# Batch 0's tokens by TensorE transposes in place of a DMA transpose, and the block sums of the second weight all on VectorE

## The chip, the cores and the metric

The kernel runs on one core of one Trainium2 chip. The metric is the device time of one execution in microseconds (us), as the median of several executions. The kernel before has 280.86 us (three executions, 280.64 to 281.7). A profiled span is about 1.8 us shorter than the measured time of the same execution (278.6 against 280.41 us before); I compare spans with spans and times with times.

## The reference

Linear attention over 8 batches, 8 heads, 576 positions and 64 columns a head, then a layer norm and a two-layer network with a residual:

```python
q_s = softmax(q, axis=-1)          # over the 64 columns of a head
k_s = softmax(k, axis=2)           # over the 576 positions
kv  = einsum('bhsd,bhse->bhde', k_s, v)
att = einsum('bhsd,bhde->bhse', q_s, kv)
x   = att.transpose(0, 2, 1, 3).reshape(8, 576, 512)
xn  = (x - mean(x)) / sqrt(var(x) + 1e-6) * g_ln
out = x + maximum(xn @ w_ch1, 0) @ w_ch2     # 512 -> 2048 -> 512
```

## The kernel before

Every instruction is entered into a plan with its engine, an estimated length, the buffers that it reads and writes, and a class. The plan then puts each engine's instructions into one fixed order.

The network works on nine groups of 512 tokens: 512 of each of the 8 batches, and the eight leftovers of 64. For each group there is a first stage, 64 matmuls of 512 columns (`xsT` by `w1`, the result rectified into `hT`), and a second stage. Batch 0's second stage is the plain product, 64 matmuls of 512 columns. From batch 1 on, seven block products of 256 columns take the place of eight; they need block sums of `hT` (called `S`) and of the second weight (called `T`). All of this fills TensorE; the softmax of the next batch runs beside it on ScalarE and VectorE, and its small matmuls (`ek` by `vb`, `eqT` by `kve`) are strewn in between.

The attention leaves x transposed (`xsT`: columns in the partitions, tokens along the row), as the first stage wants it. The statistics and the residual want tokens in the partitions. A DMA transpose makes that form:

```python
def tokens(c, cls=1, after=(), stats=()):
    ...
    i = plan.add("SP", 2.2, lambda: nc.sync.dma_start_transpose(x.rearrange("p j (k c) -> p (j k) c", k=KO1), src.rearrange("p n t -> p (n t)")),
             r=r, w=[(xk, j) for j in range(J)], mb=0.9, land=0.6, after=after)
    for j in range(J):
        ... bn_stats and bn_aggr of x[:, j, :] on VectorE
    ... 1/sqrt(var) on ScalarE, by a logarithm and an exponential
```

Batch 0's transpose is issued behind batch 1's transpose of the softmax of q (`eqT<-eq`), since transposes are kept one after the other:

```python
gate[1] = dma_t()
state["eqT"] = gate[1], tokens(0, 0.7, (gate[1],))
```

The block sums of the second weight are four kinds of subtraction. One kind (`i == 2`) runs on GpSimd and is held back by a dummy copy until batch 0's output is begun:

```python
eng, e = ("POOL", nc.gpsimd) if i == 2 else ("DVE", nc.vector)
plan.add(eng, 1.2 if i == 2 else dve_t(256 * n, 2), lambda: e.tensor_tensor(T[i][:, ks], a, b, op=ALU.subtract),
         r=r + (["hold"] if i == 2 else []), w=tk(i), cls=2, after=after if i == 2 else ())
```

The softmax here doesn't subtract the row's maximum and nothing guards it: scores larger than these inputs give would overflow.

Of the kernel before, what the change touches and what calls it, by code (L numbers as in the profile page):

```python
# [12 lines left out]
FP32 = mybir.dt.float32  # L13
FP16 = mybir.dt.float16
# [3 lines left out]
ALU = mybir.AluOpType  # L18
# [116 lines left out]
def dve_t(n, mode=1):  # L135
    return 0.15 + n / (960.0 * mode)
# [3 lines left out]
def kernel(  # L140
# [10 lines left out]
    nc = tc.nc  # L151
# [3 lines left out]
    P = 128  # L155
    J = 4
# [4 lines left out]
    KO1 = DM // P  # L161
# [8 lines left out]
    def sb(shape, dt, name):  # L170
        return persist.tile(shape, dt, name=name, tag=name)
# [12 lines left out]
    eq = [sb([P, 2, JT, P], BF16, f"eq{i}") for i in range(2)]  # L184
    eqT = [sb([P, 2 * JT, P], BF16, f"eqT{i}") for i in range(2)]
    kve = [sb([P, G, D], FP16, f"kve{i}") for i in range(2)]
    hold = sb([P, 1], FP32, "hold")
    xb = [sb([P, J, DM], FP16, f"x{i}") for i in range(3)]
    x8 = sb([P, J, DM], FP16, "x8")
    xsT = [sb([P, J * KO1, P], FP16, f"xsT{i}") for i in range(2)]  # L190
# [3 lines left out]
    ot = [sb([P, 2, DM], FP32, f"ot{i}") for i in range(NOT)]  # L194
# [5 lines left out]
    T = [sb([P, HK, 256], FP16, f"T{i}") for i in range(4)]  # L200
# [3 lines left out]
    bst = sb([P, J, 6], FP32, "bst")  # L204
# [10 lines left out]
    def nxt(what, n):  # L215
        i = cnt[what] % n
        cnt[what] += 1
        return i
# [82 lines left out]


    ident_b = sb([P, P], BF16, "ident_b")
    plan.add("POOL", 1.5, lambda: make_identity(nc, ident_b), w=["ident"])
    XK = lambda u: [("xsT", u, j, g) for j in range(J) for g in range(G)]
    SLACK = 0.8
    EK = lambda u: [("eqT", u, i) for i in range(3)]

    def attn(b, kind, between=None, exps=(), sums_=(), kvs=()):
# [152 lines left out]
        if steady:  # L462
            state["eqT"] = (dma_t(),)
        else:
            gate[1] = dma_t()
            state["eqT"] = gate[1], tokens(0, 0.7, (gate[1],))
        for hf in range(2):
            keys(hf, lk[hf])
            values(hf, lv[hf])
# [10 lines left out]
    def tokens(c, cls=1, after=(), stats=()):  # L480

        x, xk, sti, stk = xof(c)
        if c < B:
            src, r = xsT[c % 2], XK(c % 2)
        else:
            src, r = xT8, [("xT8", b, i) for b in range(B) for i in range(2)]
        i = plan.add("SP", 2.2, lambda: nc.sync.dma_start_transpose(x.rearrange("p j (k c) -> p (j k) c", k=KO1), src.rearrange("p n t -> p (n t)")),
                 r=r, w=[(xk, j) for j in range(J)], mb=0.9, land=0.6, after=after)
        for j in range(J):
            plan.add("DVE", dve_t(512), lambda j=j: nc.vector.bn_stats(bst[:, j, :], x[:, j, :]), r=[(xk, j)], w=[("bst", j)], cls=cls, slack=2.0 if c else 0.5, after=stats)  # L490
            plan.add("DVE", 0.18, lambda j=j: nc.vector.bn_aggr(bmv[:, j, :], bst[:, j, :]), r=[("bst", j)], w=[("bmv", j)], cls=cls)
        plan.add("ACT", 0.3, lambda: nc.scalar.activation(sti[:, 3, :], bmv[:, :, 1], AF.Ln, bias=eps, scale=GS * GS),
                 r=["eps"] + [("bmv", j) for j in range(J)], w=[(stk, "v", j) for j in range(J)], cls=0)
        state["rstd"] = plan.add("ACT", 0.2, lambda: nc.scalar.activation(sti[:, 4, :], sti[:, 3, :], AF.Exp, scale=-0.5),
                 r=[(stk, "v", j) for j in range(J)], w=[(stk, "r", j) for j in range(J)], cls=0)
        return i


# [58 lines left out]
        tt(3, h12, S[1][:, ks], ALU.subtract, sk(1) + hi)  # L557
        tt(2, h11, h21, ALU.subtract, lo)

    def w2_sums(k0, n, after):  # L560

        ks, kh = slice(k0, k0 + n), slice(HK + k0, HK + k0 + n)
        b11, b12 = w2_sb[:, ks, 0:256], w2_sb[:, ks, 256:512]
        b21, b22 = w2_sb[:, kh, 0:256], w2_sb[:, kh, 256:512]
        lo, hi = [("w2", k0 + i) for i in range(n)], [("w2", HK + k0 + i) for i in range(n)]
        tk = lambda i: [("T", i, k0 + j) for j in range(n)]
        def tt(i, a, b, r):
            eng, e = ("POOL", nc.gpsimd) if i == 2 else ("DVE", nc.vector)
            plan.add(eng, 1.2 if i == 2 else dve_t(256 * n, 2), lambda: e.tensor_tensor(T[i][:, ks], a, b, op=ALU.subtract),  # L569
                     r=r + (["hold"] if i == 2 else []), w=tk(i), cls=2, after=after if i == 2 else ())  # L570
        tt(0, b12, b11, lo)
        tt(1, b22, T[0][:, ks], hi + tk(0))
        tt(2, b22, b12, lo + hi)
        tt(3, b21, T[1][:, ks], hi + tk(1))
# [97 lines left out]
    def mm2(c):  # L672

        gis = [nxt("pg", 4) for _ in range(J)]
        ids = []
        steps = [(8, 1), (8, 3), (12, 1)]
        for k0 in range(0, KO2, 4):
            for j in range(J):
                def f(k0=k0, j=j):
                    for kk in range(k0, k0 + 4):  # L680
                        nc.tensor.matmul(pg[gis[j]], hT[:, kk, j * P : j * P + P], w2_sb[:, kk, :],  # L681
                                         start=(kk == 0), stop=(kk == KO2 - 1))
                i = plan.add("PE", 0.864, f, r=[("hT", kk) for kk in range(k0, k0 + 4)] + [("w2", kk) for kk in range(k0, k0 + 4)], w=[("pg", gis[j])])
                if j == 0:
                    ids.append(i)
                if (k0, j) in steps:
                    second_x(steps.index((k0, j)), (i,))
        plan.fill(ids[0], ids[-1], zeros(pg[gis[0]], False))
        evs = []
        for hf in range(2):  # L690
            o = nxt("ot", NOT)
            for i in range(2):
                j = 2 * hf + i
                ev = plan.add("DVE", dve_t(512), lambda o=o, i=i, j=j: nc.vector.scalar_tensor_tensor(  # L694
                    ot[o][:, i, :], in0=pg[gis[j]], scalar=st[c % 3][:, 4, j : j + 1], in1=xb[c % 3][:, j, :],
                    op0=ALU.mult, op1=ALU.add),
                    r=[("pg", gis[j]), (("x", c % 3), j), (("st", c % 3), "r", j)], w=[("ot", o, i)], cls=0)
                evs.append(ev)
            store(c, o, hf)
        return evs[:1]  # L700

    def zeros(bank_, start):
        def f(n):
# [36 lines left out]
    for b in range(B):  # L740
        if b:
            state["tok"] = tokens(b, 0.7, stats=state["stats"])
        if b == B - 1:
            tokens(8, 0.7, stats=state["stats"])
        ids = mm1(b, b > 0, () if b else opened)
        if b == 0:
            plan.fill(warmed, open_ids[0], zeros(pg[3], True))
            plan.fill(open_ids[-1], ids[0], zeros(pg[opened[0]], False))
        elif b < B - 1:
            attn(b + 1, "steady", None, before, (ids[0],), (ids[10],))  # L750
        before = (ids[-1], state["rstd"])
        if b == 0:
            evs = mm2(b)
            plan.add("POOL", 0.2, lambda: nc.gpsimd.tensor_copy(hold, ot[0][:, 0, :1]), r=[("ot", 0, 0)], w=["hold"])
            for k0 in range(0, HK, 2):
                w2_sums(k0, 2, evs)
        else:
            mm2_split(b)
    mm1(8, True)
    mm2_split(8)  # L760

# [35 lines left out]
```

## Time and profile before

| | before |
|---|---|
| median time | 280.86 us |
| profiled span | 278.6 us |
| TensorE busy | 270.5 us, 97% |
| VectorE busy | 198.9 us, 71% |
| GpSimd busy | 5.9 us, 2% |

TensorE's timeline of the kernel before shows where its stages begin. The columns of a timeline are start, length, engine, line and operation, output and inputs, shape, count, and in brackets the idle time before with what ended it.

```profile
24.25 1.91 PE L538 MATMUL pg<-xsT,w_sb 128*128 128x512 f16 x8 [0.38 <-DVE w_sb L288]
...
36.35 8.80 PE L681 MATMUL pg<-w_sb,hT 128*128 128x512 f16 x40
...
46.87 1.04 PE L681 MATMUL pg<-w_sb,hT 128*128 128x512 f16 x4
47.84 0.63 PE L398 MATMUL pa<-eqT,kve 64*64 64x512 bf16 x8
...
66.96 0.60 PE L618 MATMUL pg<-w_sb,hT 128*128 128x256 f16 x4
...
67.83 3.22 PE L618 MATMUL pg<-w_sb,hT 128*128 128x256 f16 x28
71.00 1.49 PE L618 MATMUL pg<-T,S 128*128 128x256 f16 x12
72.41 0.83 PE L370 MATMUL pa<-vb,ek 64*64 64x65 f16 x72
...
83.14 7.08 PE L538 MATMUL pg<-xsT,w_sb 128*128 128x512 f16 x32
```

Batch 0's second stage begins at 36.35 us, batch 1's first stage at 52.15 us (in the prediction), its second stage at 66.96 us, and batch 2's first stage at 83.14 us.

VectorE's timeline shows the wait for the tokens and what follows it:

```profile
51.31 0.69 DVE L490 BATCH_NORM_STATS2 bst<-x 128x6 f32<-128x512 f16 x1 [3.77 <-DMA x<-xsT]
...
55.21 2.73 DVE L694 SCALAR_TENSOR_TENSOR ot<-pg,st,x 128x512 f32<-128x512 f32 x4 [0.60 <-ACT st L494]
...
73.81 0.88 DVE L628 SCALAR_TENSOR_TENSOR cp<-pg,st,x 128x256 f32<-128x256 f32 x2 [0.60 <-ACT st L494]
```

The last line is the evacuation that TensorE's 1.50 us hole at 74.75 us waits for (an evacuation is VectorE's or ScalarE's copy of a result out of PSUM, the memory that TensorE writes to).

### The profile page before, as it was taken

The numbers are of one execution on the slowest core, as the hardware profiler recorded it, in microseconds if no ns is written. First come the engines' busy times: TensorE is split into PE (matmuls) and PEld (weight loads), VectorE is DVE, ScalarE is ACT, GpSimd is POOL, SyncE is SP. The second block draws the span as 40 slices with busy tenths as digits, with TensorE's granted clock in tenths as the row PEclk, the third lists the DMA queues.
The fourth block names the chain that finished last, engine by engine and source line by source line (L and its number), as shares of the span: only waits on it lengthen the run. The fifth ranks groups of instructions, "written<-read, shape, count | busy, mean of one in ns | idle before, by whom it ended". The sixth has DMA issues, their size and how long they took to land.

```text
span 278.6 us, 5657 instructions
## 1 busy us (share of the span) xinstructions
PE 270.5 (97%) x2327; PEld 164.5 (59%) x2327; DVE 198.9 (71%) x406; ACT 167.9 (60%) x273; POOL 5.9 (2%) x15
## 2 busy tenths in 40 slices
PE   8999999999799999999999999999999999999994
PEld 3444444436674478447844784478447844874583
DVE  1878896599859966976599569764996773641572
ACT  4668986499478695668566946685655077016500
POOL 1000000060000000000000000000000000000000
PEclk9999999999999999999999999999999999999999
DMA  7999999998977993579858975697543450023004
GB/s 268 362 386 387 387 390 197 266 354 217 356 229 151 227 383 64 151 165 383 125 152 154 393 125 151 142 388 144 153 85 73 80 153 0 0 49 104 0 2 152
DMA packets 57953, 55.35 MB, mean 199 GB/s; under 512 B 36676, under 2 KB 37192, under 8 KB 57928
## 3 DMA queue, kind: packets, MB, share of 16 engines
q1 hardware_dynamic: 57776, 54.86, 68.2%
q8 instruction: 18, 0.29, 0.4%
q10 hardware_dynamic: 152, 0.13, 0.1%
q14 instruction: 7, 0.06, 0.1%
HBM read 36.70 MB, written 9.44 MB: 166 GB/s over the span
## 4 chain that ended last, share of the span: by engine, by line
PE 78%; DVE 13%; DMA 6%; ACT 2%; issue 1%; SPq 0%
PE pg L538 38%; PE pg L618 32%; DMA stg<-in_moe_w_ch_dram 4%; PE pg L705 3%; DVE eq L332 2%; DMA x<-xsT 2%; DVE S L554 2%; DVE zq L328 2%; DVE bst L490 2%; PE pa L370 1%; PE pa L618 1%; PE pa L398 1%; DVE ot L694 1%; DVE T L569 1%; PE pa L282 1%
## 5 line engine op out<-in xcount | busy, mean ns | idle before, releaser
L501 ACT ACTIVATE hT<-pg 128x512 f16<-128x512 f32 x134 | 78.8, 600 | 66.6 <-PE pg L538 65.7
L538 PE MATMUL pg<-xsT,w_sb 128*128 128x512 f16 x488 | 108.2, 379 | 1.1 <-ACT hT L501 0.4
L538 PEld LDWEIGHTS <-w_sb 128*128 128x128 f16 x568 | 54.9, 98 | 66.0 <-issue 1.4
L618 PEld LDWEIGHTS <-S 128*128 128x128 f16 x512 | 49.7, 98 | 7.6 <-issue 1.5
L618 PE MATMUL pg<-T,S 128*128 128x256 f16 x368 | 42.2, 273 | 1.5 <-DVE cp L628 1.5
L618 PEld LDWEIGHTS <-hT 128*128 128x128 f16 x384 | 37.0, 98 | 8.2 <-issue 3.0
L554 DVE TENSOR_TENSOR S<-hT 128x1024 f16<-128x1024 f16 x32 | 21.8, 683 | 23.6 <-ACT hT L501 23.6
L628 DVE SCALAR_TENSOR_TENSOR cp<-pg,st,x 128x256 f32<-128x256 f32 x46 | 20.2, 479 | 13.3 <-PE pg L618 12.6
L490 DVE BATCH_NORM_STATS2 bst<-x 128x6 f32<-128x512 f16 x36 | 24.1, 671 | 7.6 <-DMA x<-xsT 7.6
L618 PE MATMUL pg<-w_sb,hT 128*128 128x256 f16 x248 | 29.4, 273 | 0.0
L628 DVE SCALAR_TENSOR_TENSOR ot<-pg,st,cp 128x256 f32<-128x256 f32 x47 | 20.5, 476 | 11.4 <-PE pg L618 11.3
L332 DVE TENSOR_TENSOR eq<-eq,rzq 128x1152 bf16<-128x1152 bf16 x16 | 22.7, 1418 | 0.5
L328 DVE TENSOR_REDUCE zq<-eq 128x18 f32<-128x1152 bf16 x16 | 21.5, 1344 | 0.3 <-ACT eq L326 0.3
L359 ACT CAST vb<-stg 128x1152 f16<-128x1152 f32 x16 | 18.7, 1169 | 4.3 <-DMA stg<-in_v_dram 4.3
L326 ACT ACTIVATE eq<-stg 128x1152 bf16<-128x1152 f32 x16 | 18.8, 1176 | 2.1 <-DMA stg<-in_q_dram 1.9
L353 ACT ACTIVATE ek<-stg 128x1152 bf16<-128x1152 f32 x16 | 18.7, 1166 | 2.2 <-DMA stg<-in_k_dram 2.2
L411 ACT CAST xsT<-pa 128x512 f16<-128x512 f32 x30 | 15.5, 600 | 3.0 <-PE pa L398 3.0
L705 PE MATMUL pg<-zero 128*128 128x512 f16 x52 | 14.6, 430 | 1.2 <-DVE zero L224 1.2
L618 PE MATMUL pg<-w_sb,S 128*128 128x256 f16 x128 | 15.3, 272 | 0.0
L618 PE MATMUL pg<-T,hT 128*128 128x256 f16 x120 | 14.4, 272 | 0.4 <-DVE ot L628 0.4
L681 PE MATMUL pg<-w_sb,hT 128*128 128x512 f16 x64 | 14.7, 380 | 0.0
L538 PE MATMUL pg<-xT,w_sb 128*128 128x512 f16 x64 | 14.0, 379 | 0.0
(64 smaller groups left out, 164.6 us busy)
## 6 DMA issues: line engine op xcount, KB each, us to landing
stg<-in_q_dram SPq DMA_DIRECT2D x16, 576.0 KB, 5.3
stg<-in_k_dram SPq DMA_DIRECT2D x16, 576.0 KB, 7.3
stg<-in_v_dram SPq DMA_DIRECT2D x16, 576.0 KB, 8.2
out_dram<-ot SPq DMA_DIRECT2D x33, 256.0 KB, 3.5
stg<-in_moe_w_ch_dram SPq DMA_DIRECT2D x16, 512.0 KB, 9.7
out_dram<-ot SPq DMA_DIRECT2D x1, 512.0 KB, 2.8
x<-xsT SPq DMA_TRANSPOSE x8, 6.9
out_dram<-ot SPq DMA_DIRECT2D x1, 128.0 KB, 2.7
```

Of the source, the lines that this page charges most:

```text
L326: plan.add("ACT", act_t(QW), lambda: nc.scalar.activation(e.rearrange("p j (s d) -> p s j d", s=2), sv(s), AF.Exp), r=sk(s), w=[("eq", u, ...
L328: plan.add("DVE", dve_t(QW), lambda: nc.vector.reduce_sum(zq[:, hf], eh, axis=AX.X), r=[("eq", u, hf)], w=[("zq", hf)], cls=qcls, after=sums_)
L332: plan.add("DVE", dve_t(QW), lambda: nc.vector.tensor_tensor(eh, eh, rzq[:, hf].to_broadcast([P, 2 * JT, D]), op=ALU.mult), r=[("rzq", hf) ...
L353: plan.add("ACT", act_t(QW), lambda: nc.scalar.activation(ek[u][:, hf].rearrange("p j (s d) -> p s j d", s=2), sv(s), AF.Exp), r=sk(s), w= ...
L359: plan.add("ACT", act_t(QW), lambda: nc.scalar.copy(vd, va), r=sk(s), w=[("vb", u, hf, i) for i in range(2)], cls=cls, slack=late, after=t ...
L490: plan.add("DVE", dve_t(512), lambda j=j: nc.vector.bn_stats(bst[:, j, :], x[:, j, :]), r=[(xk, j)], w=[("bst", j)], cls=cls, slack=2.0 if ...
L501: nc.scalar.activation(hT[:, m, :], bank, AF.Relu)
L538: nc.tensor.matmul(bank[gi], w1_sb[:, ko, m * P : m * P + P], xt[:, ko], start=(ko == 0), stop=(ko == KO1 - 1))
L554: plan.add("DVE", dve_t(256 * n, 2), lambda: nc.vector.tensor_tensor(S[i][:, ks], a, b, op=op), r=r, w=sk(i), cls=0.3 if k0 else 0.45)
L618: nc.tensor.matmul(g[i][0], fa(k, i), fb(k), start=(first and k == 0 and (i == 0 or g[0][1] != g[1][1])), stop=(last and k == HK - 1), ski ...
L628: nc.vector.scalar_tensor_tensor(dst[:, i, :], in0=g[i][0], scalar=sti[:, 4, 2 * t0 + i : 2 * t0 + i + 1], in1=src[:, i, :], op0=ALU.mult, ...
L705: nc.tensor.matmul(bank_, zero[:, :P], zero, start=start, stop=start, skip_group_check=True)
```

## The change

The intent is to have batch 0's tokens earlier. TensorE transposes `xsT` itself, 16 blocks of 128x128 inside batch 0's second stage, and VectorE copies them out of PSUM. The DMA queue is rid of one transpose. GpSimd's block sums move to VectorE, so that they no longer contend with it. The core of the diff:

```diff
+    ident_h = sb([P, P], FP16, "ident_h")
+    plan.add("POOL", 1.5, lambda: make_identity(nc, ident_h), w=["ident_h"])
...
             gate[1] = dma_t()
-            state["eqT"] = gate[1], tokens(0, 0.7, (gate[1],))
+            state["eqT"] = (gate[1],)
...
-        i = plan.add("SP", 2.2, lambda: nc.sync.dma_start_transpose(...), ...)
+        for hf in range(2) if c == 0 else ():
+            t = nxt("pa", 4)
+            v = pa[t].bitcast(FP16)
+            def f(hf=hf, v=v):
+                for n in range(8):
+                    nc.tensor.transpose(v[:, n * P : n * P + P], src[:, 8 * hf + n, :], ident_h)
+            plan.add("PE", 0.52, f, r=r + ["ident_h"], w=[("pa", t)], cls=0, after=after)
+            plan.add("DVE", dve_t(1024, 2), lambda hf=hf, v=v: nc.vector.tensor_copy(
+                x[:, 2 * hf : 2 * hf + 2, :], v.rearrange("p (j n) -> p j n", j=2)), ...)
+        if c:
+            i = plan.add("SP", 2.2, lambda: nc.sync.dma_start_transpose(...), ...)
...
-            eng, e = ("POOL", nc.gpsimd) if i == 2 else ("DVE", nc.vector)
-            plan.add(eng, ..., lambda: e.tensor_tensor(T[i][:, ks], a, b, op=ALU.subtract), ...)
+            plan.add("DVE", dve_t(256 * n, 2), lambda: nc.vector.tensor_tensor(T[i][:, ks], a, b, op=ALU.subtract), ...)
...
+                if (k0, j) == (4, 2):
+                    tokens(0, 0.7, (i,))
```

The dummy copy `hold` and its ordering are removed too. The diff also sets the plan's slack for batch 0's statistics to 0, and passes on batch 0's 1/sqrt(var) as an ordering mark from its new place; both only move instructions. Because the plan orders everything anew, other instructions than these change places as well.

More of the change, by code (lines that the diff above doesn't have):

```diff
@@ L186 @@
     kve = [sb([P, G, D], FP16, f"kve{i}") for i in range(2)]
-    hold = sb([P, 1], FP32, "hold")
     xb = [sb([P, J, DM], FP16, f"x{i}") for i in range(3)]
@@ L486, in tokens @@
             src, r = xT8, [("xT8", b, i) for b in range(B) for i in range(2)]
-        i = plan.add("SP", 2.2, lambda: nc.sync.dma_start_transpose(x.rearrange("p j (k c) -> p (j k) c", k=KO1), src.rearrange("p n t -> p (n t)")),
-                 r=r, w=[(xk, j) for j in range(J)], mb=0.9, land=0.6, after=after)
+        i = None
+        for hf in range(2) if c == 0 else ():
[6 more added lines that the diff above has]
+            plan.add("DVE", dve_t(1024, 2), lambda hf=hf, v=v: nc.vector.tensor_copy(
+                x[:, 2 * hf : 2 * hf + 2, :], v.rearrange("p (j n) -> p j n", j=2)), r=[("pa", t)], w=[(xk, 2 * hf), (xk, 2 * hf + 1)], cls=cls)
+        if c:
+            i = plan.add("SP", 2.2, lambda: nc.sync.dma_start_transpose(x.rearrange("p j (k c) -> p (j k) c", k=KO1), src.rearrange("p n t -> p (n t)")),
+                     r=r, w=[(xk, j) for j in range(J)], mb=0.9, land=0.6, after=after)
         for j in range(J):
-            plan.add("DVE", dve_t(512), lambda j=j: nc.vector.bn_stats(bst[:, j, :], x[:, j, :]), r=[(xk, j)], w=[("bst", j)], cls=cls, slack=2.0 if c else 0.5, after=stats)
+            plan.add("DVE", dve_t(512), lambda j=j: nc.vector.bn_stats(bst[:, j, :], x[:, j, :]), r=[(xk, j)], w=[("bst", j)], cls=cls, slack=2.0 if c else 0.0, after=stats)
             plan.add("DVE", 0.18, lambda j=j: nc.vector.bn_aggr(bmv[:, j, :], bst[:, j, :]), r=[("bst", j)], w=[("bmv", j)], cls=cls)
@@ L494, in tokens @@
         state["rstd"] = plan.add("ACT", 0.2, lambda: nc.scalar.activation(sti[:, 4, :], sti[:, 3, :], AF.Exp, scale=-0.5),
-                 r=[(stk, "v", j) for j in range(J)], w=[(stk, "r", j) for j in range(J)], cls=0)
+                                 r=[(stk, "v", j) for j in range(J)], w=[(stk, "r", j) for j in range(J)], cls=0)
         return i
@@ L558, in sums, with w2_sums @@
         tt(2, h11, h21, ALU.subtract, lo)
-    def w2_sums(k0, n, after):
+    def w2_sums(k0, n):
         ks, kh = slice(k0, k0 + n), slice(HK + k0, HK + k0 + n)
@@ L567, in tt @@
         def tt(i, a, b, r):
-            eng, e = ("POOL", nc.gpsimd) if i == 2 else ("DVE", nc.vector)
-            plan.add(eng, 1.2 if i == 2 else dve_t(256 * n, 2), lambda: e.tensor_tensor(T[i][:, ks], a, b, op=ALU.subtract),
-                     r=r + (["hold"] if i == 2 else []), w=tk(i), cls=2, after=after if i == 2 else ())
+            plan.add("DVE", dve_t(256 * n, 2), lambda: nc.vector.tensor_tensor(T[i][:, ks], a, b, op=ALU.subtract),
+                     r=r, w=tk(i), cls=2)
         tt(0, b12, b11, lo)
@@ L688, in mm2 @@
         plan.fill(ids[0], ids[-1], zeros(pg[gis[0]], False))
-        evs = []
         for hf in range(2):
@@ L693, in mm2 @@
                 j = 2 * hf + i
-                ev = plan.add("DVE", dve_t(512), lambda o=o, i=i, j=j: nc.vector.scalar_tensor_tensor(
+                plan.add("DVE", dve_t(512), lambda o=o, i=i, j=j: nc.vector.scalar_tensor_tensor(
                     ot[o][:, i, :], in0=pg[gis[j]], scalar=st[c % 3][:, 4, j : j + 1], in1=xb[c % 3][:, j, :],
@@ L697, in mm2 @@
                     r=[("pg", gis[j]), (("x", c % 3), j), (("st", c % 3), "r", j)], w=[("ot", o, i)], cls=0)
-                evs.append(ev)
             store(c, o, hf)
-        return evs[:1]
     def zeros(bank_, start):
@@ L744 @@
             tokens(8, 0.7, stats=state["stats"])
+        rstd = state.get("rstd")
         ids = mm1(b, b > 0, () if b else opened)
@@ L750 @@
             attn(b + 1, "steady", None, before, (ids[0],), (ids[10],))
-        before = (ids[-1], state["rstd"])
         if b == 0:
-            evs = mm2(b)
-            plan.add("POOL", 0.2, lambda: nc.gpsimd.tensor_copy(hold, ot[0][:, 0, :1]), r=[("ot", 0, 0)], w=["hold"])
+            mm2(b)
+            rstd = state["rstd"]
             for k0 in range(0, HK, 2):
-                w2_sums(k0, 2, evs)
+                w2_sums(k0, 2)
         else:
             mm2_split(b)
+        before = (ids[-1], rstd)
     mm1(8, True)
```

## The prediction

> **What bounds the kernel now.** I read the page's busy shares first, then TensorE's timeline for its holes, then the chain of waits through those holes, then the SyncE queue's timeline.
>
> The page says that TensorE is the bound of the whole:
>
> ```profile
> PE 270.5 (97%) x2327; PEld 164.5 (59%) x2327; DVE 198.9 (71%) x406; ACT 167.9 (60%) x273; POOL 5.9 (2%) x15
> ```
>
> 270.5 of 278.6 us are busy. From 83 us to 274.8 us the chain of waits consists of TensorE pieces alone, so nothing that VectorE or the DMA queue gains there is worth time. Only the first 83 us can give something. Since "busy" hides spacing, I compared issue times: the 24 matmuls of batch 0's second stage from 39.80 to 45.07 us are 0.22 us apart, as densely as 512 columns go anywhere in this trace. So that stage, from 36.35 to about 52.15 us, has no slack either. The holes come after it (start, length, engine, line and operation, output and inputs, count, idle time before it with its releaser):
>
> ```profile
> 52.15 3.62 PE L538 MATMUL pa<-xsT,w_sb 128*128 128x512 f16 x16
> 56.02 3.61 PE L538 MATMUL pg<-xsT,w_sb 128*128 128x512 f16 x16 [0.25 <-DVE ot L694]
> 60.05 7.07 PE L538 MATMUL pg<-xsT,w_sb 128*128 128x512 f16 x32 [0.42 <-ACT hT L501]
> ...
> 74.75 1.91 PE L618 MATMUL pg<-T,S 128*128 128x256 f16 x16 [1.50 <-DVE cp L628]
> ...
> 81.11 1.91 PE L618 MATMUL pg<-T,hT 128*128 128x256 f16 x16 [0.41 <-DVE ot L628]
> ```
>
> The four sum to 0.25 + 0.42 + 1.50 + 0.41 = 2.58 us: that is the whole prize, 0.9% of the time. The chain of waits shows where they come from (start, length, what):
>
> ```profile
> 45.34 5.95 DMA x<-xsT
> 51.29 0.02 issue
> 51.31 0.71 DVE bst L490
> ...
> 55.21 2.73 DVE ot L694 x4
> 57.94 1.27 DVE zq L328
> 59.21 0.02 issue
> 59.23 0.28 DVE rzq L330
> 59.51 0.02 issue
> 59.53 2.35 DVE eq L332
> ...
> 73.81 0.89 DVE cp L628 x2
> 74.70 0.04 issue
> 74.75 5.41 PE pg L618 x48
> ```
>
> Batch 0's tokens land at 51.29 us by a DMA transpose that starts only at 45.34 us, because the SyncE queue issues it behind batch 1's transpose of eq. VectorE's timeline has 3.77 us of idle time before that landing. After it VectorE is packed to 73.2 us: statistics, batch 0's output, batch 2's softmax, block sums, batch 1's statistics. The 1.50 us hole is that string arriving late. The 0.25 us is the first bank that batch 0's output frees. The 0.42 us is ScalarE, whose queue stood behind the statistics' logarithm (54.64 us) before it could empty batch 1's first banks.
>
> **What the Trainium skill says.** Four places bear on this.
> (1) "VectorE: DVE Perf Modes", section on the three transpose paths: a 128x128 transpose takes 390 ns on TensorE and 1309 ns by the DMA crossbar. In a stream this trace is far below that: nine transposes of batch 0's eq start at 9.57 us and the next group at 10.17 us, 0.067 us each; the second nine take 16.00 to 16.51 us, 0.057 us each. The DMA transpose of x, 16 such blocks, took 5.95 us, or 0.37 us each. I use the trace.
> (2) The same page, "Why PSUM operands drop a tier": 16-bit copies out of PSUM reach the 2x mode at most. The trace agrees with 2x: 128x1024 bf16 out of PSUM took 0.69 us, below the 1.07 us of one element a cycle at the 0.96 GHz that the page gives.
> (3) "SBUF — State Buffer", "Who interferes with whom": a VectorE instruction with two SBUF inputs contends with GpSimd reads. The trace agrees: the same 128x1152 multiply took 2.35 us at 59.53 us, while GpSimd did its four block sums (56.17 to 60.67 us), and 1.36 us at 63.48 us after them.
> (4) "TensorE: Matmul & The Clock Gate", Part 4, says that transpose mode does not count as work for the clock. A pass of 1 us is short, and the granted clock stayed 1.00 through the eq transposes; I count nothing for it.
>
> **The change part by part.**
> *Removed:* one DMA transpose of x (1.84 us of SyncE issue at 45.34 us, 5.95 us to landing), four GpSimd subtractions of 1.16 us, and the small GpSimd copy that held them back. The next q loads move up by 1.84 us, from 47.23 us.
>
> *Added on TensorE:* 16 transposes. The built order puts all 16 in one run right after batch 1's second key-value product, which ends at 46.87 us, between matmuls of the dense second stage. Nothing hides them: 16 x 0.057 to 0.067 = 0.9 to 1.07 us, say 1.0 us. Their banks were read by then (the ScalarE scaling of the second bank, 46.30 + 0.31 us).
>
> *Added on VectorE:* two copies of 128x1024, started 0.61 us apart = 1.2 us, and four 128x512 subtractions at 0.39 us = 1.6 us. Two of the four go ahead of key-value work, where VectorE has the 3.77 us of idle time.
>
> *VectorE step by step.* In the new order, the key-value scalings of batch 1 end about 47.6 us as now. The first 8 transposes are done by then, so copies run 47.6 to 48.9. The four statistics pairs took 51.31 to 54.61 = 3.3 us: now to 52.2. Two leftover subtractions fill ScalarE's 0.5 us for the logarithm and exponential. Batch 0's output starts about 52.95 instead of 55.21: 2.3 us earlier. It ends 55.6. Softmax of batch 2 follows; the first multiply is 1.36 instead of 2.35 us, another 1.0 us. So VectorE reaches the block sums at about 64.75 - 2.3 - 1.0 = 61.5 us. There it is too early: the first block sum needs the ninth hT tile. Batch 1's first stage starts at 52.15 + 1.0 = 53.15 us and makes a tile in 0.866 us (four matmuls), so the ninth is out at 60.9 and copied by about 62.3. Then 4 x 0.66 for the sums and 2.4 for three statistics pairs: 67.3. The last hT tile is due at 53.15 + 16 x 0.866 = 67.0, copied 67.6. Four sums and the last statistics pair (3.5 us) end about 71.2; 0.55 us on ScalarE; the evacuation 0.9 us: about 72.7, against 74.70 now.
>
> *When TensorE wants it.* The stage after starts at 67.0 us, as before (66.96): what transposes push back, the two small holes give back. It has 48 matmuls x 0.109 = 5.2 us and 0.8 us of key-value work before it needs that evacuation: 73.0. So the 1.50 us hole closes with 0.3 us to spare. The hole of 0.41 us is untouched: there TensorE waits for an evacuation of what it has just finished, and the order at that spot is the same.
>
> *Sum:* holes closed 0.25 + 0.42 + 1.50 = 2.17 us; transposes +1.0 us; net -1.17 us. I leave 0.1 us for a hole that closes only in part. 280.86 - 1.07 = 279.8 us.
>
> **Rivals.**
> (a) *The transposes cost what they save.* If they run at 0.14 us each, with bank switches and a wait for the copies, they are 2.2 us and the time stays at 280.9. For it: they stand on the bound engine, and batch 1's later products reuse their banks after VectorE's copies. Against: 18 like them took 1.1 us in this trace, and between transposes and reuse stand eight matmuls of 0.22 us and another group, about 2 us, while the copies need 1.4 us after.
> (b) *ScalarE takes the place of the removed wait.* In the new order both exponentials of q come early, but an exponential of k stands ahead of hT evacuations and needs its load. The SyncE queue issues those loads behind batch 1's transpose of x, which waits for token tiles that TensorE now makes about 1 us later. In the trace that issue alone took 3.57 us, and k landed 4.8 us after its own. I get k at 60.5 to 61 us, when ScalarE reaches it at about 59.8. The free banks cover some 2 us. If it slips 1 us further, TensorE stalls 0.5 to 1 us and half the gain is gone: 280.3.
> (c) *Everything closes, cheaper transposes.* With 0.9 us of transposes and the 0.41 us hole gone too, the limit is 280.86 - 2.58 + 0.9 = 279.2 us.
> (d) *The gain of 3.3 us on VectorE carries to the end.* This would be 277.5. Against: TensorE has only 2.58 us of holes to give.
>
> **Range and chances.** Between (c) and (a) lie 279.2 and 280.9; runs of the kernel before spread by 1 us, so I take 278.9 to 281.0 as eight in ten, centred at 279.8. A change of 2% is 5.6 us. Faster by that much would need twice the holes there are; slower by that much would need a new stall or lost clock that nothing shows. I give each 1%.
>
> **What would show it right or wrong.** In the new profile: 16 transposes about 46.9 to 47.9 us with no idle time before them; batch 0's statistics starting near 48.9 and its output near 53.0 us; both multiplies of batch 2 at 1.36 us; no GpSimd work after the start; the holes of 0.25, 0.42 and 1.50 us gone and that of 0.41 us there; the stage of batch 1 still starting near 67 us and everything after 83 us about 1.1 us earlier. The prediction is wrong if the transposes are spaced over 0.1 us, if a wait of ScalarE on k (or of its v copies, which precede the statistics' logarithm) opens a new hole in TensorE between 57 and 75 us, or if the first 24 us shift: a second identity on GpSimd comes ahead of the small one, but the w1 loads, which run at 387 GB/s, set the pace there.

## The result, and the profile after

The changed kernel took 279.16 us in the median (279.03 to 279.41, four executions), beside 280.87 us of the kernel before in the same rounds: 1.71 us less. Its ratio is 0.9935, with a 95% interval of 0.9913 to 0.9956. A ratio is the mean time of one kernel's fast runs over that of the other's of the same rounds, so it is not quite the ratio of the medians. All outputs were correct, here and in every experiment.

The page of the kernel after gives TensorE's share, and the shares of the chain that ended last:

```profile
PE 271.0 (98%) x2342; PEld 165.3 (60%) x2342; DVE 200.9 (72%) x412; ACT 168.6 (61%) x273; POOL 1.7 (1%) x12
...
PE 93%; DMA 4%; ACT 1%; DVE 1%; issue 0%
```

The same chain line of the kernel before:

```profile
PE 78%; DVE 13%; DMA 6%; ACT 2%; issue 1%; SPq 0%
```

VectorE's share of the chain falls from 13 to 1%: the string of VectorE work between 51 and 75 us no longer sets the end. GpSimd has only its start-up work left.

TensorE's timeline of the kernel after, with the stage starts, the transposes, and the one hole that is left after the start:

```profile
24.67 1.90 PE L550 MATMUL pg<-xsT,w_sb 128*128 128x512 f16 x8 [0.83 <-DVE w_sb L287]
...
36.77 8.80 PE L692 MATMUL pg<-w_sb,hT 128*128 128x512 f16 x40
...
47.29 1.07 PE L494 MATMUL pa<-ident_h,xsT 128*128 128x128 f16 x16
48.19 1.03 PE L692 MATMUL pg<-w_sb,hT 128*128 128x512 f16 x4
49.15 0.41 PE L399 MATMUL pa<-eqT,kve 64*64 64x512 bf16 x4
...
50.46 0.41 PE L399 MATMUL pa<-eqT,kve 64*64 64x512 bf16 x4
...
53.69 3.62 PE L550 MATMUL pa<-xsT,w_sb 128*128 128x512 f16 x16
57.15 10.52 PE L550 MATMUL pg<-xsT,w_sb 128*128 128x512 f16 x48
67.51 3.66 PE L629 MATMUL pg<-w_sb,hT 128*128 128x256 f16 x32
...
71.97 0.80 PE L371 MATMUL pa<-vb,ek 64*64 64x65 f16 x72
72.70 2.79 PE L629 MATMUL pg<-T,S 128*128 128x256 f16 x24
...
79.95 1.91 PE L629 MATMUL pg<-T,hT 128*128 128x256 f16 x16 [0.41 <-DVE ot L639]
...
81.98 8.38 PE L550 MATMUL pg<-xsT,w_sb 128*128 128x512 f16 x38
```

And VectorE's timeline of the kernel after:

```profile
47.95 1.29 DVE L496 COPY x<-pa 128x1024 f16<-128x1024 f16 x2
49.15 0.68 DVE L502 BATCH_NORM_STATS2 bst<-x 128x6 f32<-128x512 f16 x1
...
53.04 2.73 DVE L706 SCALAR_TENSOR_TENSOR ot<-pg,st,x 128x512 f32<-128x512 f32 x4
...
57.36 1.36 DVE L333 TENSOR_TENSOR eq<-eq,rzq 128x1152 bf16<-128x1152 bf16 x1
...
71.17 0.88 DVE L639 SCALAR_TENSOR_TENSOR cp<-pg,st,x 128x256 f32<-128x256 f32 x2 [0.60 <-ACT st L506]
```

The statistics begin at 49.15 in place of 51.31 us, without a wait. The output begins at 53.04 in place of 55.21, and the multiply takes 1.36 in place of 2.35 us. The evacuation runs from 71.17 to 72.05 us, and TensorE goes on with the block products at 72.70 us, straight after key-value work: the 1.50 us hole is gone.

The stage lengths, each a difference of two starts in the timelines, tell where the time went:

| stage | before | after | difference |
|---|---|---|---|
| start mark to batch 0's second stage (24.25 to 36.35; 24.67 to 36.77) | 12.10 | 12.10 | 0.00 |
| batch 0's second stage (to 52.15; to 53.69) | 15.80 | 16.92 | +1.12 |
| batch 1's first stage (to 66.96; to 67.51) | 14.81 | 13.82 | -0.99 |
| batch 1's second stage (to 83.14; to 81.98) | 16.18 | 14.47 | -1.71 |
| all that follows, to the last evacuation (274.84; 273.61) | 191.70 | 191.63 | -0.07 |
| sum | 250.59 | 248.94 | -1.65 |

I call this sum the work between the marks: from the first matmul after TensorE's wait at 24 us to the start of VectorE's last evacuation, which is the last piece of the chain of waits. What lies before the first mark is set by the loads of the first weight and differs from profile to profile: the mark stood at 24.67, 24.87 and 24.73 us in three profiles of the same changed kernel, with 0.83, 0.32 and 1.15 us of idle time ahead of it. What lies behind the second mark, the end, was 3.76 us before and 3.79 us after (a span is given to 0.1 us, so an end is good to 0.05 us). So the spans differ by 1.65 - 0.42 - 0.03 = 1.20 us, and the median times by 1.71 us; the profiled execution of the kernel before (280.41 us) was 0.45 us quicker than its median.

### The profile page after: what moved, and what is told of

Its sections match the earlier page's. It is cut to its first block, busy times and chain, and to the rows that moved or that the text cites. A ratio compares the mean times of both kernels' runs of the same rounds, so it can differ in the third digit from the quotient of the medians.

```text
span 277.4 us, 5694 instructions
## 1 busy us (share of the span) xinstructions
PE 271.0 (98%) x2342; PEld 165.3 (60%) x2342; DVE 200.9 (72%) x412; ACT 168.6 (61%) x273; POOL 1.7 (1%) x12
## 4 chain that ended last, share of the span: by engine, by line
PE 93%; DMA 4%; ACT 1%; DVE 1%; issue 0%
PE pg L550 43%; PE pg L629 35%; PE pg L692 5%; DMA stg<-in_moe_w_ch_dram 4%; PE pg L715 3%; PE pa L371 2%; PE pa L629 1%; PE pa L399 1%; PE pa L550 1%; PE pa L281 1%; DVE ot L639 0%; PE pa L422 0%; ACT w_sb L268 0%; ACT eq L327 0%; PE pa L494 0%
## 5 line engine op out<-in xcount | busy, mean ns | idle before, releaser
L333 DVE TENSOR_TENSOR eq<-eq,rzq 128x1152 bf16<-128x1152 bf16 x16 | 21.7, 1357 | 0.5
```

Of the source, the lines that this page charges most:

```text
L333: plan.add("DVE", dve_t(QW), lambda: nc.vector.tensor_tensor(eh, eh, rzq[:, hf].to_broadcast([P, 2 * JT, D]), op=ALU.mult), r=[("rzq", hf) ...
```

## The experiments

My theory was that the transposes on TensorE bring the whole gain and that the move of the sums only removes contention that no longer matters. Its rivals were that the sums' move brings a good part of it, that an earlier DMA transpose would do as well, and that the gain is only spread of the start. The ratios below are each against the kernel before in the same rounds, and "work" is the work between the marks.

| run | median us | ratio (95% interval) | work us | end us |
|---|---|---|---|---|
| changed kernel, first result | 279.16 | 0.9935 (0.9913 to 0.9956) | 248.94 | 3.79 |
| x0, changed kernel again | 278.99 | 0.9936 (0.9924 to 0.9948) | 248.94 | 3.79 |
| x1, transposes only | 280.29 | 0.9983 (0.9971 to 0.9995) | 248.95 | 4.83 |
| x2, sums only | 280.63 | 1.0001 (0.9981 to 1.0021) | 249.79 | 4.22 |
| x3, transposes twice | 280.10 | 0.9976 (0.9964 to 0.9988) | 249.85 | 3.75 |
| x4, transposes only, padded | 279.06 | 0.9910 (0.9884 to 0.9936) | 248.56 | 3.77 |
| x5, sums only, padded | 279.66 | 0.9938 (0.9913 to 0.9962) | 249.68 | 3.77 |
| x6, sums only, x by DMA first | 282.18 | 1.0023 (0.9986 to 1.0059) | 251.03 | 4.94 |
| x7, transposes early | 279.60 | 0.9931 (0.9907 to 0.9954) | not comparable | 3.75 |
| y1, before, padded | 280.57 | 0.9986 (0.9971 to 1.0001) | 250.41 | 3.76 |
| y2, x4 again | 279.10 | 0.9928 (0.9912 to 0.9944) | 248.55 | 3.79 |
| y3, changed kernel again | 279.26 | 0.9934 (0.9920 to 0.9948) | 248.96 | 3.81 |

x0 to x3 share their rounds, x4 to x7 share others, and y1 to y3 a third set. The medians of the kernel before were 280.83, 281.59 and 281.06 us there, so medians of different sets should not be compared to better than half a microsecond.

### x0: the changed kernel again

> The changed kernel once more, for the size of the gain beside the others and for the start: its hole at 24 us was 0.83 us in the first profile against 0.38 us in the kernel before. If that comes of the changed start (second identity, later g) it is 0.8 us again; if it is the spread of the w1 loads it will differ. Time: 279.2 us, ratio to before 0.9935 give or take 0.002.

It took 278.99 us. The work was the same to 0.01 us, and the hole at the start was 0.32 us instead of 0.83. So the size of the start hole is not fixed by the change. But the first mark stood between 24.67 and 24.87 us in the three profiles of the changed kernel, and at 24.25 and 24.23 us in the two profiles of the kernel before (one is y1's, below). That the change makes the start later by up to half a microsecond is not ruled out by the profiles; the medians speak against it, since they differ by no less (1.71 us) than the work does (1.65 us).

### x1: the transposes alone

The changed kernel, with one kind of block sum back on GpSimd behind the dummy copy:

```diff
-            plan.add("DVE", dve_t(256 * n, 2), lambda: nc.vector.tensor_tensor(...), r=r, w=tk(i), cls=2)
+            eng, e = ("POOL", nc.gpsimd) if i == 2 else ("DVE", nc.vector)
+            plan.add(eng, 1.2 if i == 2 else dve_t(256 * n, 2), lambda: e.tensor_tensor(...),
+                     r=r + (["hold"] if i == 2 else []), w=tk(i), cls=2, after=after if i == 2 else ())
```

> Only the TensorE transposes; a quarter of w2's block sums stays on GpSimd behind batch 0's output. My theory: the time is set by TensorE's issue, and VectorE in the changed kernel has over 1 us to spare before TensorE needs batch 1's first evacuation, so the slowed multiply (2.35 for 1.36 us) is absorbed: 279.2 us, as the changed kernel. Rival (removing GpSimd's contention is a good part of the gain): 279.7 us or more, with a hole of 0.5 us or more near 73 us.

The time missed that: 280.29 us, only 0.17% below the kernel before. The work did not miss it: 248.95 us, the same as with both parts. VectorE's timeline of this run shows the contention back and absorbed:

```profile
57.10 2.35 DVE L334 TENSOR_TENSOR eq<-eq,rzq 128x1152 bf16<-128x1152 bf16 x1
...
71.25 0.88 DVE L641 SCALAR_TENSOR_TENSOR cp<-pg,st,x 128x256 f32<-128x256 f32 x2 [0.60 <-ACT st L507]
```

The multiply takes 2.35 us again, yet the evacuation comes at 71.25 against 71.17 us, because there was slack in between: the first block sum starts 0.73 us later than in the changed kernel (62.32 against 61.59), but in the changed kernel VectorE then waits 0.32 us for `hT`, and by the second set of sums the two runs are only 0.1 us apart (68.43 against 68.33). (x1's first mark, 24.42 us, is 0.25 us earlier, so counted from the marks each of these differences is 0.25 us larger.) TensorE goes on with the block products at 72.25 us, without a hole. The microsecond was lost elsewhere: the end took 4.83 us. The DMA view of x1 from 274 to 279 us has one instruction fetch among the last stores, and the last store needs 3.3 us to land:

```profile
q14 instruction: 1, 0.01, 0.4%
...
out_dram<-ot ACTq DMA_DIRECT2D x1, 128.0 KB, 3.3
```

The packet records say how: an 8192-byte fetch starts at 275.79 us, the store's last packet of 1024 bytes starts only at 276.09 us when the fetch is over, and all its other data packets had started by 275.75 us. That suggested a test: x1 without the fetch at this place. (That x1's work equals the changed kernel's to 0.01 us is partly chance: its order saves 0.39 us up to 83 us, as x4 shows below, and loses as much at 112 us, where a later x lands late and a hole of 0.25 us opens.)

### x4: the transposes alone, with the fetch moved

x1 with three more clears of a tiny tile on VectorE at the start. They do nothing, but shift VectorE's instruction stream:

```diff
-        plan.add("DVE", 0.1, lambda: nc.vector.memset(eps, 1e-6 * GS * GS), w=["eps"])
+        def eps_again():
+            for _ in range(4):
+                nc.vector.memset(eps, 1e-6 * GS * GS)
+        plan.add("DVE", 0.1, eps_again, w=["eps"])
```

> x1_transposes_only with three more memsets of the 128x1 eps tile at the start of VectorE, so that VectorE runs as many instructions as the changed kernel. In x1's profile TensorE's work from the hole at 24 us to VectorE's last evacuation took 248.95 us, as in the changed kernel (248.94 us in both profiles), but from that evacuation to the end of the span it took 4.83 us against 3.79 us; the DMA view shows an 8 KB instruction fetch at 275.8 us, in front of the last packets of the last store, where the changed kernel's last such fetch is at 270.5 us. Theory: the fetch's place follows the count of instructions; with three more it moves to about 270.5 us, the end takes 3.8 us again, and the time is 279.1 us, as the changed kernel. Rival (GpSimd's contention or the other order costs this time in the work itself): 280.3 us as x1.

It held: 279.06 us. The same view of x4, from 274 to 279 us, has no fetch at all, and its last store lands in 2.2 us:

```profile
q1 hardware_dynamic: 268, 0.35, 19.6%
q10 hardware_dynamic: 144, 0.13, 7.8%
issues: line engine op xcount, KB each, median us to landing
...
out_dram<-ot ACTq DMA_DIRECT2D x1, 128.0 KB, 2.2
```

The end shrank from 4.83 to 3.77 us; the last fetches of 8192 bytes now start at 261.9 and 270.0 us. Of the 1.06 us, 0.43 us is the late packet: from the store's first packet to its last record it took 0.96 us in x1 and 0.53 us in x4. The remaining 0.6 us lies between that record and the end of the span (2.07 against 1.44 us), and the trace doesn't show what it is.

The work is 248.56 us, another 0.39 us less than in the changed kernel. TensorE's timeline of x4 shows why:

```profile
49.06 0.63 PE L403 MATMUL pa<-eqT,kve 64*64 64x512 bf16 x8
...
77.59 0.63 PE L403 MATMUL pa<-eqT,kve 64*64 64x512 bf16 x8
78.14 1.48 PE L634 MATMUL pg<-w_sb,S 128*128 128x256 f16 x12
79.46 1.91 PE L634 MATMUL pg<-T,hT 128*128 128x256 f16 x16
```

Two stages are shorter. Batch 0's second stage takes 16.69 us (36.68 to 53.37), 0.23 us less than in the changed kernel: the query products (`eqT,kve`) stay in one run of eight, as in the kernel before, where the changed kernel has two runs of four. Batch 1's second stage takes 14.31 us (67.18 to 81.49), 0.16 us less: the plan put the query products ahead of 12 other matmuls, so the last product no longer waits 0.41 us for the evacuation, though the 40 matmuls from 72.41 us take 0.2 us more than 40 like them in the changed kernel. Both come from the order that the plan happened to choose, not from GpSimd's work.

### x2 and x5: the sums alone, without and with the fetch moved

The kernel before, with all sums on VectorE; x5 adds four clears on VectorE and three copies of one element a partition on ScalarE:

```diff
-            eng, e = ("POOL", nc.gpsimd) if i == 2 else ("DVE", nc.vector)
-            plan.add(eng, ..., lambda: e.tensor_tensor(T[i][:, ks], a, b, op=ALU.subtract), ...)
+            plan.add("DVE", dve_t(256 * n, 2), lambda: nc.vector.tensor_tensor(T[i][:, ks], a, b, op=ALU.subtract), ...)
...
-            plan.add("POOL", 0.2, lambda: nc.gpsimd.tensor_copy(hold, ot[0][:, 0, :1]), ...)
```

> Only the block sums all on VectorE; the DMA transpose of batch 0's x stays. My theory: x still lands near 51.3 us, so the holes of 0.25 and 0.42 us stay; the string behind it is 1.0 us shorter by the multiply, so the hole of 1.50 us shrinks to about 0.5 us; no cost on TensorE: 279.9 us. Rival (the transposes do all of it): 280.9 us. Rival (the sums do all of it and the transposes only cost): 279.2 us or less.

x2 showed no gain in time (280.63 us), though its work was 0.80 us less than before. Its end was 4.22 us, with a fetch at 276.76 us among the last packets. Here no packet of the store is late: the last one comes 2.3 us after the second mark, as in the changed kernel, and the added 0.4 us lies between it and the end of the span. With the fetches moved:

> x2_sums_only with four more such memsets on VectorE and three 128x1 copies on ScalarE at the start. In x2's profile TensorE's work between the same two marks took 249.79 us, 0.80 us less than the kernel before (250.59 us), yet the time was only 0.2 us less, with an end of 4.22 us against 3.76 us and an instruction fetch at 276.8 us. Theory: with the fetches moved earlier the end takes 3.8 us and the time is 280.0 us, 0.8 us under the kernel before. Rival (the sums alone are worth nothing): 280.7 us.

x5 took 279.66 us, somewhat less than expected, with 249.68 us of work, 0.91 us less than before. TensorE's timeline of x5:

```profile
74.00 1.91 PE L625 MATMUL pg<-T,S 128*128 128x256 f16 x16 [0.92 <-DVE cp L635]
...
80.37 1.91 PE L625 MATMUL pg<-T,hT 128*128 128x256 f16 x16 [0.41 <-DVE ot L635]
```

The tokens still come late: VectorE's statistics begin at 51.57 us. The 1.50 us hole shrinks to 0.92 us instead of going. Batch 1's two stages together take 29.86 us (52.53 to 82.39) against 30.99 us before: 1.13 us less, about the 0.99 us by which the multiply is shorter. Batch 0's second stage takes 16.08 us, 0.28 us more than before, because here too the plan splits the query products into two runs of four (x2: 16.03 us). So each part does something alone: -0.8 to -0.9 us of work by the sums, -1.6 to -2.0 us by the transposes. Together they do -1.65 us. The sums add nothing once the tokens come early, because the hole they shrink is then closed.

The times support this less well than the work does. By its ratio, 0.9938, x5 cannot be told from the changed kernel, and of the 0.87 us between the spans of x2 and x5 (278.66 and 277.79 us) only about 0.4 us is the end, while 0.34 us is the start. But within their common rounds every execution of x5 (279.58 us and more) was slower than every one of x4 (279.47 us and less).

### x3: the transposes twice

```diff
-                for n in range(8):
+                for n in [*range(8), *range(8)]:
```

> The changed kernel with each of the 16 transposes done twice into the same place (result unchanged). My theory: they stand on TensorE's dense stage, nothing hides them, and 16 more take 16 x 0.056 = 0.9 us: 280.1 us. Rival (they fill time in which TensorE would have waited anyway): 279.2 us. Rival (VectorE's copies are the path): more than 280.6 us, with a hole behind the copies.

It held: 280.10 us. TensorE's timeline of x3:

```profile
47.22 1.96 PE L494 MATMUL pa<-ident_h,xsT 128*128 128x128 f16 x32
```

The work grew by 249.85 - 248.94 = 0.91 us for 16 more transposes. That is 0.057 us each, and all of it shows in the end: nothing hides them in this stage.

### x6: an earlier DMA transpose in their place

x2 with batch 0's transpose of x issued ahead of batch 1's transpose of eq:

```diff
-            gate[1] = dma_t()
-            state["eqT"] = gate[1], tokens(0, 0.7, (gate[1],))
+            tok0 = tokens(0, 0.7, (gate[1],))
+            gate[1] = tok0
+            gate[1] = dma_t()
+            state["eqT"] = gate[1], tok0
```

> x2_sums_only with the DMA transpose of batch 0's x issued ahead of batch 1's transpose of eq, and no TensorE transposes. Theory: what counts for VectorE's string is only when x lands; here it lands about 3 us earlier (near 48 us instead of 51.8) at no cost on TensorE, but eq's transpose now lands behind it, past 49 us, where TensorE's in-order stream wants it at about 49.3 us; the holes of 0.25, 0.42 and 1.50 us close in the main and a new one of up to 1 us opens behind eq's landing: 279.0 to 280.0 us. Rival (the place in the queue is worth nothing): 280.6 us. Rival (eq's delay costs more than the string gains): over 281 us.

The slower way came true: 282.18 us. The tokens do come early (the statistics begin at 46.85 us), but eq comes late. SyncE's queue and then TensorE in x6:

```profile
38.26 6.59 SPq L489 DMA_TRANSPOSE x<-xsT  x1
44.95 2.75 SPq L337 DMA_TRANSPOSE eqT<-eq  x1
```

```profile
51.40 0.63 PE L398 MATMUL pa<-eqT,kve 64*64 64x512 bf16 x8 [2.15 <-DMA eqT<-eq]
...
83.32 0.22 PE L421 MATMUL pa<-eqT,kve 64*64 64x64 bf16 x2 [0.74 <-ACT xsT L411]
```

In x5 eq's transpose is issued at 42.67 us. Here it stands behind x's until 44.95 us, TensorE waits 2.15 us for it, and two further small holes open at 83 us. The 1.50 us hole is closed, but the work is 0.44 us above that of the kernel before. In addition two fetches at 278.1 us lengthen the end to 4.94 us. A second path beside the queue, and not merely an earlier place in it, is what the transposes on TensorE give. This is argued from x6 alone; a DMA transpose of x issued from another engine's queue was not tried.

### x7: the transposes in the hole at the start

The changed kernel, with the transposes right behind batch 0's last rows, where TensorE waits for the first weight, and the copies given a high class:

```diff
-                x[:, 2 * hf : 2 * hf + 2, :], v.rearrange("p (j n) -> p j n", j=2)), ..., cls=cls)
+                x[:, 2 * hf : 2 * hf + 2, :], v.rearrange("p (j n) -> p j n", j=2)), ..., cls=-0.5)
...
-                if (k0, j) == (4, 2):
-                    tokens(0, 0.7, (i,))
...
         if blk == 1:
-            rest()
+            tokens(0, 2.5, (rest(),))
```

> The changed kernel with its 16 transposes moved from the dense second stage to the place right behind batch 0's last rows in TensorE's order, where TensorE waits 0.3 to 1.1 us for the centred w1 block, and the two copies ahead of other work there; statistics stay late. Theory: the transposes fall into that hole and cost nothing, their 0.9 us and the group switches (0.2 us) leave the path, and the new order of batch 1's products closes the hole of 0.41 us too: about 277.8 us. Rival (VectorE's two copies, 1.2 us, delay the centring of w1 that TensorE waits for): 279.0 us or more, with a longer hole between 24 and 30 us.

It missed by 1.8 us: 279.60 us, no better than the changed kernel. The timelines of x7, TensorE first and VectorE second:

```profile
23.91 1.07 PE L495 MATMUL pa<-ident_h,xsT 128*128 128x128 f16 x16
...
30.82 3.63 PE L551 MATMUL pg<-xsT,w_sb 128*128 128x512 f16 x16 [0.66 <-DVE w_sb L287]
34.69 3.63 PE L551 MATMUL pg<-xsT,w_sb 128*128 128x512 f16 x16 [0.24 <-DVE w_sb L287]
```

```profile
25.09 1.28 DVE L497 COPY x<-pa 128x1024 f16<-128x1024 f16 x2
...
30.35 1.29 DVE L287 TENSOR_TENSOR w_sb<-w_sb,cp 128x512 f16<-128x512 f16 x2
...
34.22 1.28 DVE L287 TENSOR_TENSOR w_sb<-w_sb,cp 128x512 f16<-128x512 f16 x2
```

The transposes fill idle time now, but the two copies and a changed order on VectorE delay the centring of the weight (`w_sb<-w_sb,cp`): its second to last round is at 30.35 us (28.09 us in the changed kernel) and its last at 34.22 us (30.68 us). TensorE waits twice for it, and batch 0's second stage begins at 38.16 instead of 36.77 us. That stage is then 16.21 instead of 16.92 us long, and the 0.41 us hole is closed as expected, which doesn't win it back. (Its work is not comparable because the transposes lie before the first mark.) So VectorE, not TensorE, makes the spot at 24 us dear. I did not try whether copies at other places would do better.

### y1: the kernel before with its fetches moved

If a fetch can cost a microsecond, part of the change's own gain could be a fetch moved by accident. The kernel before has late fetches too, at 277.2 and 280.0 us. y1 is the kernel before with seven clears on VectorE and three small copies on ScalarE, which gives it the instruction counts of the kernel after on these two engines.

> The kernel before with seven more clears of eps on VectorE and three copies of one element a partition on ScalarE in its first microseconds: its instruction counts there become those of the kernel after, nothing else. Theory: in the kernel before the late instruction fetches lie in the last microseconds or behind the last packets of the last store and already cost nothing (its end, from the start of the last evacuation, is 3.8 us as in the kernel after); the fetches move forward to about 262 and 271 us, the work between the marks stays 250.6 us, the end 3.75, ratio 0.997 to 1.003. Rival: part of the change's 1.7 us is only such a fetch moved: then this kernel is 0.5 to 1 us faster than before (ratio about 0.997 or below) although its work between the marks is the same.

Its fetches moved to 263.4 and 271.5 us: the end was 3.76 us as before, the work 250.41 us, the ratio 0.9986 with 1 inside the interval. The small holes of TensorE differ too: those of 0.25 and 0.42 us are no longer listed, and one of 0.23 us (a wait for `S`) stands at 70.87 us; batch 1's two stages together take 30.88 us against 30.99 us. So the work of the kernel before is known to some 0.2 us only, and so are the gains that are counted from it. The expectation held. In the kernel before, the fetch at 277.20 us starts behind the store's last record at 277.17 us, and the other after the span; they cost nothing. So the gain of the change is not a moved fetch. A small effect, up to the 0.3% of the interval's lower end, is not ruled out by the times; the work and the end say there is none.

### y2 and y3: transposes alone against both parts, side by side

The kernel of x4 and the changed kernel, unedited, in the rounds of y1:

> The same kernel as in the padded run of the transposes alone (block sums on GpSimd as before), beside the changed kernel in the same rounds. Theory: the work between the marks is 248.6 us against 248.95, because batch 1's order happens to close the 0.41 us hole too; 0.3 to 0.4 us faster than the changed kernel, ratio 0.992. Rival: what was seen is the spread of the start, and both are equal within 0.1%.

> The changed kernel once more, for comparison in these rounds: 248.95 us between the marks, end 3.8, ratio 0.9935 as measured twice.

The work is 248.55 against 248.96 us, as expected, and the spans are 276.8 and 277.5 us. The times are 279.10 and 279.26 us with ratios of 0.9928 and 0.9934, whose intervals overlap almost wholly. So it is shown that the transposes alone are not slower than both parts together. That they are faster by 0.4 us is to be seen in the profiles, but not settled by the times, since the start varies by as much.

## Why the prediction was right or wrong

The time, 279.16 us, is in the range, and the class "within 2%" is right. The mechanism was right; the gain of 1.71 us was under-forecast at 1.07 us. Step by step:

- **Removed and added work, VectorE's steps.** The prediction had the copies at 47.6, the statistics at 48.9, the output at 52.95 and the block sums at 61.5 us. They came at 47.95, 49.15, 53.04 and 61.59 us. It had the evacuation done at about 72.7 us; that was 72.05. But the first mark of the new profile is 0.42 us later. Counted from the marks, these five came earlier than forecast by 0.07, 0.17, 0.33, 0.33 and 1.07 us. So the rule "find the string that ends in the wait, and move it by what its head moves" worked to a third of a microsecond as far as the block sums. The rest was mis-sized: behind the last `hT` tiles the prediction had four sums and a statistics pair (3.5 us), but in the new order three sums and one aggregation were left (68.33 to 70.57 us). The stage after it began at 67.51 us, 67.09 us without the later mark, against 67.0 us forecast.
- **The cost of the transposes.** "Say 1.0 us" was 0.90 us for the run itself (47.29 to 48.19), and x3 confirmed 0.91 us for 16. But the stage grew by 1.12 us. The other 0.22 us is the order around them: after the change the query products come in two runs of four matmuls in place of one run of eight. By the starts in the two timelines the runs take 0.34 + 0.34 in place of 0.55 us, and the eight matmuls beside them 0.97 + 0.97 in place of 1.83 us. The prediction had read the new order for the transposes only. This split does not come with the transposes: x1 and x4, which have the transposes alone, keep the run of eight, and their stage grew by 0.89 us; x2 and x5, which have the sums alone, split it, and theirs grew by 0.23 and 0.28 us without any transpose. (x6 moves the sums and keeps the run, so it is the plan's order and not the sums as such.)
- **The holes.** This is the step that was mis-sized: "holes closed 0.25 + 0.42 + 1.50 = 2.17 us". The first two were worth 0.99 us (14.81 to 13.82 us of stage) and reported 0.67; batch 1's second stage gave 1.71 us, of which the third hole reported 1.50. That is 2.70 us in all. The Trainium skill, "Perfetto Trace Analysis", "Summary: the profiler window per engine type", says that TensorE's end is an estimate, that is, modelled and not observed. The trace agrees that a reported end cannot be used as a slot: in the kernel after, 16 matmuls reported as 3.62 us from 53.69 us are followed by the next at 57.15 us, 3.46 us later. An idle time measured from a reported end leaves out that overlap of 0.16 us. For the first two holes that is the difference: their 16 matmuls took 3.87 and 4.03 us to the next start in the kernel before, and 3.46 and 3.45 us after. The third hole was worth 1.61 us, 0.11 more than reported: the key-value run in front of it took 2.34 us to the next start (72.41 to 74.75), and 0.73 us after (71.97 to 72.70). The last 0.10 us is a fourth hole that the timeline does not list: the 28 matmuls from 67.83 us take 3.17 us, where 32 like them take 3.49 us after the change, which makes 3.05 us for 28. In y1, the same kernel with its fetches moved, a wait of 0.23 us for `S` is listed at that place. So 0.16 + 0.16 + 0.11 + 0.10 us is the whole difference between 2.70 and 2.17.
- **The reserve.** The 0.1 us for a hole closed only in part was not needed. With the measured terms, 1.12 - 0.99 - 1.71 = -1.58, and -0.07 in all the rest, the sum is -1.65 us.
- **The 0.41 us hole.** It stayed, as forecast (79.95 us).
- **Rival (a)**, transposes that cost what they save: wrong, 0.057 us each. **Rival (b)**, a stall of ScalarE on k: it didn't occur; between 20 and 85 us the only waits listed on TensorE are the start's 0.83 and the 0.41 us. **Rival (c)**, everything closed for 279.2 us: the time fits, but by luck, since the 0.41 us hole was still there and the others were larger than it counted. **Rival (d)**: wrong, as argued.
- **The two parts.** The prediction counted 2.3 us of earlier tokens and 1.0 us of a shorter multiply in one string and did not say which was needed. x1 and x4 show that the first alone closes all three holes. The second is worth 0.8 to 0.9 us of work (0.73 us for x5 if y1 is taken as the kernel before) only where the first is missing; beside the first it cost 0.22 us, by the split of the query products.

What stays open: why the end lengthens by 0.6 us in x1 and 0.4 us in x2 beyond any late packet when a fetch falls into it, why the plan splits the query products, and what sets the start between 24.2 and 24.9 us.

## What to carry to other kernels

Where one engine bounds the whole, add up the differences between the starts of its stages, not the idle times that a profile reports: each of the three holes here was worth 0.11 to 0.16 us more than it said, a fourth was not listed, and the transposes added to a dense stage cost their full issue time. When two changes feed the same wait, test each alone: here the first closed the hole and took the whole gain, and the other one could be dropped. And before you believe a difference of under half a per cent, look at the start and the end of the program, since a loss of 1 us there hid most of the gain of x1.

## What the Trainium skill lacked or had wrong

- "VectorE: DVE Perf Modes", "The three transpose paths", gives 390 ns for a 128x128 transpose on TensorE. "TensorE: Matmul & The Clock Gate", "Part 4: PE-mode transpose", gives about 275 ns in one kernel's context. In a stream of 16 they took 0.90 us, 0.056 us each, and 16 more added 0.91 us. Neither passage says what a transpose takes in a stream. For back-to-back matmuls of 128 columns the second page has 55.6 ns; that transposes follow one another as densely, as here, it doesn't say.
- The first of these pages gives 1309 ns for the DMA crossbar. A transfer of 16 blocks took 5.95 us to landing, 0.37 us a block. What mattered more was its place in the queue: eq's transpose, issued 2.3 us later in x6 than in x5, made TensorE wait 2.15 us.
- "Runtime: NRT & Kernel Launch", "Instruction fetch mechanics", calls the cost of a fetch mostly hidden. The runs agree for most fetches, but one that fell among the last packets of the last store lengthened that store from 2.2 to 3.3 us and the end by 1.06 us (x1 against x4). Which fetch does so depends on a handful of instructions. The page also speaks of 16 KiB blocks; here the fetch records of one queue are of 16384 bytes (18 in the kernel before) and those of another, the late ones among them, of 8192 bytes (7).
- "Perfetto Trace Analysis" says that TensorE's end is estimated, but not what that does to idle times: holes reported as 0.25, 0.42 and 1.50 us were worth 0.41, 0.58 and 1.61 us.
